# One written list of 1117 steps in place of a list of 547 steps and a scheduled rest

## The chip, the cores and the metric

The kernel runs on one core of one Trainium2 chip. The metric is device time in microseconds (us) from one run of the program. The core has five engines that work side by side, each in the order of its own instructions: TensorE (PE in the profile; its weight loads are PEld), VectorE (DVE), ScalarE (ACT), GpSimd (POOL) and SyncE (SP), which here only issues transfers (DMAs). An instruction that waits for another engine holds up what is behind it on its own engine.

## The reference, cut to what matters

A delta-rule attention over 4 batches, 8 heads, 768 tokens and 48 features feeds a feed-forward network (FFN) without a nonlinearity. The heads' outputs, side by side, are the 384 features of 3072 tokens.

```python
k_n = k / (np.linalg.norm(k, axis=-1, keepdims=True) + 1e-06)
for t in range(S):
    y[:, :, t] = q[:, :, t] @ state
    v_old = state.T @ k_n[:, :, t]
    state = state + beta[t] * outer(k_n[:, :, t], v[:, :, t] - v_old)
x = y.transpose(0, 2, 1, 3).reshape(3072, 384)
out = ((x @ w1) * (x @ w2)) @ w3 @ w_out
```

(The products over batch and head are written short here.) The weights arrive as 64-bit floats, 1024 wide in the hidden dimension; q, k, v and beta as 32-bit floats.

## The kernel before, in words

The tokens are cut into twelve chunks (m, c) of 64; two chunks make a pair (j, u). Within a chunk the recurrence is solved at once by a triangular inverse, and only a 48 x 48 state goes from chunk to chunk. The work is cut into parts, each a generator that yields after the instructions of one engine (they are collected in `parts`, L739 and following). A call of `step(name)` (L777) runs a part up to its next yield, so one step is the work of one engine. The parts, with the lines that the profile names:

- k, q, v: load the keys, queries and values of a chunk (L173); p: load keys and queries once more, with features in other partitions (L190, sixteen DMAs in two steps); beta: loads and transposes beta.
- K, Q: for chunks 0 and 1, transposes on PE (L275) with copies to KQ (L285, L287). d: for the later chunks the same on DVE (L263).
- g and N: squares of the keys on POOL and their sums on DVE (L212, L214), then the norms (fifteen small DVE instructions, L220 to L243), once a pair.
- s: the products of keys with keys and queries (L300), written out as U (DVE, L309) and PT (L327). u: stores U in 32 x 32 blocks in DRAM (Ud, L343).
- V: the inverse of a pair's blocks. POOL clears the result (L351), SP loads the blocks (Ub, L355), 31 steps of two DVE instructions follow (L369, L374), and SP stores the result (Vd, L382). For pair 0 the result lies in PSUM meanwhile, with copies on ACT.
- e: the corner. Four loads from Vd (L387), a transpose on DVE (L399), two groups of small matmuls (L408, L422) with copies on ACT (L415, L429).
- n: values times norms on POOL (L438). c: the chain of a chunk, three groups of PE products (all at L452), each followed by a DVE step: the residual R (L484), X (L494) and the next state S (L512). y: the outputs (L547), copied on ACT to xT (L568), and for odd chunks six DMAs within xT (L579).
- P: a piece of weights. SP loads it (L592), ACT works on it twice (L600, L601), DVE twice (L603, L604), POOL once (L608). P0 to P7 are w_out, P8 to P23 w3, P24 to P35 w1 and w2. t transposes w3 (L643), f folds w3 and w_out into one matrix w34 (L652).
- a: an eighth of the hidden dimension for a pair's 512 tokens (128 of each batch): product with w1 on PE (L672), copy on ACT (L681), product with w2 on PE (L672), elementwise product on DVE (L686). o: a batch's outputs, PE (L692), ACT (L698), store by SP (L701).

A part name carries its indices: a13 is pair 1, eighth 3; o02 is pair 0, batch 2; V2 is pair 2; P22 is a piece.

What sets the order: the string ORDER names 547 steps. They hold all weight pieces, transposes and folds, chunks 0 to 3, the scores and block stores of chunks 4 and 5, the inverses V0 to V2, and pair 0's a and o steps. After them `in_text_order` (L132) ties each instruction to the one before it on its engine, so these instructions keep the order of the text on each engine. The rest, chunks 4 to 11 and the FFN blocks of pairs 1 to 5, is emitted by loops with `finish`, and the tile framework's scheduler orders those instructions by its own priorities, behind the listed ones on SP's queue (`tc.issue_after(last)`). In these loops a chunk is followed by the next chunk's values and corner, after an even chunk by the whole preparation of the pair after the next and its inverse, and then by up to six FFN parts that are ready (`emit(6)`); a pair's eight a and four o parts come up once its second chunk is out. The framework adds the waits between engines from the tiles that instructions read and write, in both cases.

Buffers that tie steps together go around in fixed turns (`in_turn`): three PSUM banks for the FFN, folds and transposes (ps_f), two double banks for scores, chain and outputs (ps_w), one for the corners (ps_t), five raw buffers shared by weight pieces and the first half of a, ten slabs shared by w3, its transposes and ab, two xT.

Of the kernel before, what the change touches and what calls it, by code (L numbers as in the profile page):

```python
# [39 lines left out]
Q1 s0 Q1 g0 g0 P11 P10 t2 N0 s0 s0 s0 k2 g1 P6 s0 P6 P6 Q1 P11 P14 P14 Q1 P14 n0 t3 P6 t3  # L40
t14 P13 s0 s0 P13 P13 P14 s1 P13 s1 s1 s1 s1 s1 p2 p2 d2 P23 P23 P23 P23 d2 d2 g1 d2 P4 P4
P4 P15 u0 P4 P15 P15 P2 P2 u1 P2 t2 P7 P7 V0 V0 V0 P7 P7 t5 V0 V0 V0 P12 P12 s1 t5 p3 P12 t6
V0 V0 V0 V0 V0 V0 V0 V0 t14 V0 V0 V0 s2 t6 t15 t15 P17 g1 g1 V0 V0 V0 V0 V0 V0 V0 V0 V0 P2
f3 p3 P12 f1 f1 f1 k3 P15 t7 t7 P29 P29 P17 V0 V0 P21 V0 V0 V0 V0 s1 V0 f3 V0 f3 P16 P16 P16
s0 f7 f7 v1 f7 t4 t4 f2 f2 P21 P21 g1 P16 t8 g1 P8 V0 V0 V0 P17 P17 t9 f2 g1 P29 P29 t8 f4
P8 P8 g1 e0 e0 n0 d3 e0 P18 N1 s2 s2 s2 s2 V1 e0 e0 t9 e0 n1 n1 e1 P18 P21 t13 t13 s2 P8 t0
t0 e1 P19 P19 P20 c0 c0 e1 e1 d3 P26 P26 v3 d3 c0 c0 d3 y0 P25 y0 f4 f4 e1 P26 P26 P18 P18
c1 c1 P24 u2 P19 s3 P20 P20 t10 t10 e1 s3 s3 s3 s3 s3 f5 P19 P25 P24 P24 P20 t12 t12 P27 t11
# [2 lines left out]
P34 P28 P32 P32 P34 a03 a01 v2 V1 V1 V1 V1 V1 V1 a03 c1 a02 a01 V1 V1 g2 P32 P28 V1 P30 a03
a03 a02 a02 a02 P28 n2 V1 V1 V1 V1 V1 g2 g2 P28 P33 n3 k5 n3 a00 a01 a01 P35 p4 g2 g2 g2 a06
a00 V1 V1 V1 V1 e2 e3 n2 a06 a04 a04 a07 c1 c2 P35 P35 P33 P33 P33 a00 e2 d4 d4 P35 g2 N2 e2
e2 a04 a04 a00 e2 c2 e3 p5 d4 d4 a07 a07 a07 a06 a06 e2 s4 e3 s4 s4 s4 s4 a05 a05 a05 c2 s4
e3 e3 V2 e3 c2 c2 c2 a05 y2 y2 d5 d5 c3 p5 d5 d5 o02 c3 s5 s5 s5 o02 c3 s5 s5 u4 u5 o01 c3
# [792 lines left out]
```

## Time and profile before

| What | Value |
|---|---|
| median of 3 runs | 678.1 us (675.17 to 681.01) |
| the profiled execution's own time | 674.21 us |
| its span, first to last instruction | 672.5 us |
| mean granted clock of TensorE | 0.949 |
| busy time of PE, DVE, ACT, POOL | 597.1, 355.5, 163.2, 103.3 us |
| first FFN product (L672) starts | 142.97 us |
| last matmul ends | 668.8 us |

The trace is of one execution on the chip. A busy PE is not a PE at its peak, for matmuls overlap and their ends are modelled; what PE costs is better seen in the time from one group to the next. The granted clock is the share of full speed that the chip's throttle gave to TensorE. In a row of groups stand the line, engine, operation, output and inputs, the shape, the count, then the busy time and the mean of one in nanoseconds, then the idle time ahead of it and what ended it. The chain of waits follows the end of the program back, at each step to what released it.

### The profile page before, as it was taken

Reading aid. Unit: us, or ns where it says so; the run is one execution under the profiler, and the core shown is the slowest. Engines: PE = TensorE matmul, PEld = TensorE weight load, DVE = VectorE, ACT = ScalarE, POOL = GpSimd, SP = SyncE. Lnnn points to the kernel's source line nnn. Section 1 sums busy time; section 2 is a strip of 40 time slices with the busy share of each in tenths; the row PEclk is TensorE's granted clock in tenths of the full one; section 3 lists DMA queues with packets and bytes.
Section 4 is the critical chain, followed back from the end, with each engine's and each line's share of the span. In section 5 each row is a group of like instructions: output and inputs, shape, how many; then the busy total and the mean of one; then the engine's idle time right before and its main releaser. Section 6 shows DMA issues by size and latency. Waiting matters only on the chain.

```text
span 672.5 us, 17051 instructions
## 1 busy us (share of the span) xinstructions
PE 597.1 (89%) x7372; PEld 353.6 (53%) x7372; DVE 355.5 (53%) x764; ACT 163.2 (24%) x333; POOL 103.3 (15%) x114
## 2 busy tenths in 40 slices
PE   2627889979797999999779989999899999999997
PEld 2524467634356644556733556544656455554454
DVE  3788987789754593343497243792537822100100
ACT  2663455531312111210101220212202122201100
POOL 6374152333300102000110001100000000000000
PEclk9986977989999999899679999999899997999999
DMA  9988664786530408214551342515133020010000
GB/s 211 225 192 179 171 159 95 174 147 127 98 52 4 106 13 160 36 20 74 127 82 46 53 65 65 129 26 96 29 66 92 39 38 2 14 36 12 0 13 36
DMA packets 201835, 55.61 MB, mean 83 GB/s; under 512 B 191968, under 2 KB 195040, under 8 KB 201760
## 3 DMA queue, kind: packets, MB, share of 16 engines
q1 hardware_dynamic: 197600, 53.74, 39.1%
q10 hardware_dynamic: 4160, 0.79, 0.7%
q8 instruction: 58, 0.95, 0.6%
q14 instruction: 17, 0.14, 0.1%
HBM read 42.30 MB, written 11.01 MB: 79 GB/s over the span
## 4 chain that ended last, share of the span: by engine, by line
PE 68%; DVE 15%; DMA 6%; issue 4%; SPq 3%; ACT 2%; POOL 1%; ACTq 0%; DVEq 0%
PE ps_f L672 29%; PE ps_f L692 16%; PE ps_w L452 7%; DVE Vb L374 4%; PE ps_w L547 4%; DVE tb L369 4%; PE ps_f L652 4%; PE ps_w L300 3%; DMA ktok<-in_k_dram 2%; PE ps_t L422 2%; PE ps_t L408 2%; SPq L190 2%; DMA Ud<-U 1%; DVE w L603 1%; DVE ab L686 1%
## 5 line engine op out<-in xcount | busy, mean ns | idle before, releaser
L672 PE MATMUL ps_f<-xT,w1s 128*128 128x512 f32 x288 | 141.3, 626 | 11.5 <-DMA xT<-xT 9.6
L672 PE MATMUL ps_f<-xT,w2s 128*128 128x512 f32 x288 | 136.2, 605 | 0.2 <-DVE ab L686 0.2
L692 PE MATMUL ps_f<-w,ab 128*128 128x384 f32 x384 | 127.6, 489 | 0.0
L686 DVE TENSOR_TENSOR ab<-a,ps_f 128x512 f32<-128x512 f32 x48 | 32.7, 684 | 127.0 <-PE ps_f L672 127.0
L692 PEld LDWEIGHTS ps_f<-w,ab 128*128 128x128 f32 x384 | 72.0, 190 | 50.1 <-issue 2.9
L672 PEld LDWEIGHTS ps_f<-xT,w1s 128*128 128x128 f32 x288 | 55.1, 198 | 77.8 <-issue 64.5
L672 PEld LDWEIGHTS ps_f<-xT,w2s 128*128 128x128 f32 x288 | 54.2, 193 | 64.4 <-issue 62.5
L681 ACT COPY a<-ps_f 128x512 f32<-128x512 f32 x48 | 28.0, 586 | 185.2 <-PE ps_f L672 169.6
L369 DVE TENSOR_TENSOR tb<-Vb,Ub 128x31 f32<-128x31 f32 (+15 forms) x155 | 57.5, 371 | 15.2 <-DMA Ub<-Ud 11.0
L374 DVE TENSOR_TENSOR Vb<-Vb,tb 128x31 f32<-128x31 f32 (+15 forms) x155 | 60.6, 391 | 4.5
L438 POOL TENSOR_TENSOR vtok<-vtok,n 128x384 f32<-128x384 f32 x24 | 20.4, 868 | 196.2 <-DMA vtok<-in_v_dram 146.8
L568 ACT COPY xT<-ps_w 48x256 f32<-48x256 f32 x96 | 30.5, 366 | 74.6 <-PE ps_w L547 74.2
L652 PE MATMUL ps_f<-w2s,w3T 128*128 128x384 f32 x128 | 45.0, 503 | 2.4 <-ACT w3T L646 1.4
L698 ACT COPY osb<-ps_f 128x384 f32<-128x384 f32 x24 | 11.5, 479 | 121.2 <-PE ps_f L692 101.5
L300 PE MATMUL ps_w<-KQ 48*64 48x128 f32 x768 | 32.0, 315 | 6.0 <-ACT PT L321 4.9
L309 DVE TENSOR_TENSOR U<-ps_w,wt 128x512 f32<-128x512 f32 x24 | 16.4, 686 | 38.6 <-PE ps_w L300 38.4
L212 POOL TENSOR_TENSOR sq<-ktok 128x384 f32<-128x384 f32 x24 | 21.4, 894 | 89.5 <-DVE ss L214 33.9
L494 DVE TENSOR_TENSOR X<-ps_w,wt 128x384 f32<-128x384 f32 x24 | 12.3, 552 | 42.6 <-PE ps_w L452 42.6
L652 PEld LDWEIGHTS ps_f<-w2s,w3T 128*128 128x128 f32 x128 | 24.2, 196 | 19.1 <-ACT w3T L646 2.2
L300 PEld LDWEIGHTS ps_w<-KQ 48*64 48x64 f32 x768 | 26.8, 158 | 11.7 <-issue 5.5
L452 PEld LDWEIGHTS ps_w<-R,TT 64*64 64x64 f32 x704 | 23.7, 143 | 10.0 <-issue 3.2
L452 PE MATMUL ps_w<-R,TT 64*64 64x48 f32 x704 | 25.5, 227 | 1.1 <-DVE R L484 1.1
(83 smaller groups left out, 574.7 us busy)
## 6 DMA issues: line engine op xcount, KB each, us to landing
raw<-in_moe_w_dram SPq DMA_DIRECT2D x16, 512.0 KB, 5.0
vtok<-in_v_dram SPq DMA_DIRECT2D x24, 192.0 KB, 4.9
raw<-in_moe_w_dram SPq DMA_DIRECT2D x24, 192.0 KB, 4.3
out_dram<-osb SPq DMA_DIRECT2D x24, 192.0 KB, 2.0
ktok<-in_k_dram SPq DMA_DIRECT2D x22, 192.0 KB, 4.0
raw<-in_moe_w_out_dram SPq DMA_DIRECT2D x8, 384.0 KB, 5.7
Ud<-U SPq DMA_DIRECT2D x48, 64.0 KB, 1.9
Ub<-Ud SPq DMA_DIRECT2D x6, 512.0 KB, 3.5
```

The source lines that it names most:

```text
L212: pool.tensor_tensor(out=sq[:], in0=kt[:, r], in1=kt[:, r], op=ALU.mult)
L300: pe.matmul(ps[half(z), h % 2, 128 * (h // 2) : 128 * (h // 2) + 128], lhsT=x[:, 0, :], rhs=x.rearrange("p j t -> p (j t)"), start=True, s ...
L369: dve.tensor_tensor(out=tv, in0=V[:, 0 : s + 1, s : s + 1].to_broadcast([P, s + 1, n]), in1=U[:, s, s + 1 : BS].unsqueeze(1).to_broadcast( ...
L374: dve.tensor_tensor(out=o, in0=o, in1=tv, op=ALU.subtract)
L452: pe.matmul(out(ps, r, h, z), lhsT=lhs(r, h, z), rhs=rhs(r, h, z), start=True, stop=True,)
L547: i = pe.matmul(region(h, z, r), lhsT=lhs, rhs=rhs, start=part[n] not in part[:n], stop=part[n] not in part[n + 1 :],)
L568: act.copy(out=xT[f, p:NP:2, b : b + NR, cc, :].rearrange("p a r t -> p r a t"), in_=pyv[f, z, b : b + NR],)
L652: pe.matmul(ps[:, 0:DM], lhsT=w3Ts[jc, kc // 4][:, kc % 4 * P : kc % 4 * P + P], rhs=wo[:, kc], start=(kc == 0), stop=(kc == KF - 1),)
L672: pe.matmul(ps[:], lhsT=w[:, m, js], rhs=x[:, m].rearrange("p b c t -> p (b c t)"), start=(m == 0), stop=(m == KM - 1),)
L681: act.copy(out=a[:], in_=ps[:])
L686: dve.tensor_tensor(out=t[:], in0=a[:], in1=ps[:], op=ALU.mult)
L692: pe.matmul(ps[:, 0:DM], lhsT=abs_[u, jc][:, b * P : (b + 1) * P], rhs=w34[:, jc, :], start=(jc == 0), stop=(jc == KF - 1),)
```

## The change

The list ORDER grows from 547 to 1117 steps and now names every step of every part, all twelve chunks, all inverses and all FFN blocks of all six pairs. The loops behind it, the helpers `finish` and `emit` and the rule that put the scheduled instructions behind the listed ones on SP's queue are gone. `in_text_order` runs as before, now over the whole program. The part functions are not touched. The first steps are not the old list's first steps either: the order of weight pieces, loads, inverses and folds is another from the start, and a and o parts no longer run whole one after another: a part's two products can lie far apart, with other parts' products or a chunk's steps between them.

```diff
 ORDER = """
-V0 P22 P1 k0 g0 K0 q0 P22 P22 P22 P1 P1 P1 g0 P3 g0 K0 P3 P3 k1 P3 K0 K0 K0 P0 g0 g0 P0 P0
-P0 P5 P5 beta Q0 Q0 Q0 Q0 Q0 P5 P5 v0 K1 K1 K1 K1 K1 g0 P10 P10 beta beta P10 P11 P11 q1 Q1
...
-t11 c1 c1 P27 f5 f5 P25 P25 y1 P9 P24 P9 P9 u3 V1 P27 P31 V1 V1 V1 V1 f6 P9 V1 V1 V1 V1 P34
-V1 V1 P27 y1 P30 t1 t1 f0 P31 V1 V1 k4 g2 V1 y1 V1 f6 P31 P31 f6 P32 P30 P30 p4 f0 f0 P34
...
-o02 V2 V2 V2 V2 V2 V2 o00 c3 o01 o00 o00 V2 V2 V2 V2 V2 o01 c3
+P6 P2 P10 k0 K0 q0 P6 P6 P2 P2 g0 g0 K0 P6 P10 P10 g0 g0 K0 K0 K0 P2 k1 K1 K1 P3 P3 P3 q1 K1
+K1 K1 P4 P4 P4 beta beta beta g0 g0 P11 P11 P11 P10 g0 g0 N0 P4 P11 Q0 Q0 Q0 P3 Q0 Q0 p2 Q1
...
+c1 e1 c1 c1 P26 P29 P29 u3 V1 k4 V1 V1 P29 f0 t11 V1 V1 V1 V1 t9 t9 P24 s1 y1 c1 f0 P27 P27
+P27 v2 n2 V1 V1 V1 V1 V1 y1 f4 P30 P30 P25 f5 f5 P32 P29 P27 f4 f4 P32 y1 g2 P30 P31 V1 c1
...
+e3 v5 e3 g2 g2 P34 N2 s4 n5 s4 P34 P34 a05 a05 c2 c2 P35 a06 s4 s4 s4 p5 p5 e3 e3 c2 c2 y2
...
+g3 a04 c3 c3 a06 n4 y3 y3 o01 o01 V2 u5 V2 V2 o00 o00 V2 V2 V2 V2 V2 V2 V2 V2 y3 a11 a11 V2
+a13 a17 a17 g3 o00 k7 V2 o01 V2 V2 V2 V2 p6 g3 V2 V2 a13 V2 V2 V2 g3 g3 V2 V2 a17 a17 V2 V2
+g3 a13 a13 a16 a16 V2 V2 d6 d6 p7 V2 V2 V2 V2 V2 o02 o02 V2 e4 e5 d6 N3 o03 o03 o03 a10 e4
...
+a10 a15 a15 u6 u7 V3 V3 a12 a12 a12 a12 y5 y5 c5 y5 o02 o12 o12 o12 V3 V3 V3 V3 V3 n6 n6 V3
+o10 o10 V3 V3 V3 V3 c5 k9 V3 d8 d8 a20 a20 o13 o13 V3 V3 V3 a24 a24 k8 V3 o10 V3 V3 g4 d8 v7
+V3 V3 V3 a27 a27 o11 o11 a22 V3 V3 a23 a23 V3 V3 V3 V3 V3 V3 a22 V3 V3 V3 e6 e6 e6 e7 c6 g4
...
+v8 V4 V4 o21 V4 V4 V4 V4 V4 V4 V4 V4 V4 V4 V4 V4 o21 V4 o22 a37 o22 a37 a34 a34 V4 V4 k10 g5
+a35 V4 V4 o21 g5 g5 V4 g5 g5 o20 o20 p10 V4 V4 V4 V4 V4 p10 V4 o22 g5 a35 o23 o23 V4 V4 V4
+V4 V4 e8 e8 a36 a36 e8 c7 c8 a35 a35 e8 e8 a31 o23 n8 o20 n8 c8 e8 e9 e9 a31 a31 a31 e9 e9
...
+V5 V5 V5 o32 o32 V5 V5 V5 V5 V5 V5 o32 V5 a47 o31 a41 V5 V5 o31 o31 a44 a44 a41 a45 a45 s11
+V5 V5 o33 o33 o33 n11 n11 a42 V5 V5 V5 V5 a42 a43 V5 V5 V5 V5 V5 V5 V5 o30 V5 V5 V5 V5 o30
+a43 e10 c9 e10 e11 e11 o30 e10 a44 e10 e10 e10 c9 c10 c10 a45 a45 c10 c10 a44 e11 e11 a46
...
+o51 o51 o51 o50 o50 o50 o52 o52 o52
 """
...
-    def finish(*names):
-        for name in names:
-            if name not in running:
-                running[name] = parts[name]()
-            for _ in running[name]:
-                pass
...
     in_text_order()
-    last = [i for i in nc.cur_bb.bb.instructions if i.engine == mybir.EngineType.SP][-1]
...
-    with tc.issue_after(last):
-        finish("e4")
-        for c in range(4, NCH):
-            finish(f"n{c}", f"c{c}", f"y{c}")
-            if c + 1 < NCH:
-                finish(f"v{c + 1}", f"e{c + 1}")
...
-            emit(6)
...
-        emit(len(units))
```

More of the change, by code (lines that the diff above doesn't have):

```diff
@@ L37 @@
 ORDER = """
-V0 P22 P1 k0 g0 K0 q0 P22 P22 P22 P1 P1 P1 g0 P3 g0 K0 P3 P3 k1 P3 K0 K0 K0 P0 g0 g0 P0 P0
-P0 P5 P5 beta Q0 Q0 Q0 Q0 Q0 P5 P5 v0 K1 K1 K1 K1 K1 g0 P10 P10 beta beta P10 P11 P11 q1 Q1
[L40 to L48, printed above, removed]
-t11 c1 c1 P27 f5 f5 P25 P25 y1 P9 P24 P9 P9 u3 V1 P27 P31 V1 V1 V1 V1 f6 P9 V1 V1 V1 V1 P34
@@ L50 @@
-V1 V1 P27 y1 P30 t1 t1 f0 P31 V1 V1 k4 g2 V1 y1 V1 f6 P31 P31 f6 P32 P30 P30 p4 f0 f0 P34
[L51 to L55, printed above, removed]
@@ L56 @@
-V2 V2 V2 V2 V2 V2 V2 V2 V2 V2 V2 v4 s5 V2 y3 y3 y3 V2 V2 V2 V2 V2 V2 V2 V2 o03 o03 o03 V2 V2
-o02 V2 V2 V2 V2 V2 V2 o00 c3 o01 o00 o00 V2 V2 V2 V2 V2 o01 c3
+P6 P2 P10 k0 K0 q0 P6 P6 P2 P2 g0 g0 K0 P6 P10 P10 g0 g0 K0 K0 K0 P2 k1 K1 K1 P3 P3 P3 q1 K1
+K1 K1 P4 P4 P4 beta beta beta g0 g0 P11 P11 P11 P10 g0 g0 N0 P4 P11 Q0 Q0 Q0 P3 Q0 Q0 p2 Q1
+Q1 Q1 s0 s0 s0 s0 s0 s0 Q1 Q1 t3 P7 P7 P7 P7 s0 P12 s1 s1 s1 s1 s1 s1 s1 p2 P12 d2 d2 t2 d2
+d2 P14 P22 P15 u0 P15 P12 P12 t4 u1 V0 P22 P22 P0 P14 P14 P14 t3 P15 P0 P0 V0 V0 V0 V0 V0
@@ new lines @@
+P22 t14 V0 V0 V0 V0 t4 t2 P5 P5 P1 P1 v0 P5 t6 t6 P15 t7 V0 p3 P1 P0 P1 P13 n0 V0 V0 V0 n0
+t14 V0 V0 V0 V0 P13 P13 V0 f1 P5 f1 f1 k2 g1 g1 g1 t7 V0 V0 V0 s0 f3 f3 P13 V0 f3 V0 V0 V0
+P23 p3 P23 t5 P23 P23 t5 P21 k3 P8 P8 V0 P21 g1 f2 f2 t15 t15 P20 P20 V0 V0 V0 P9 V0 V0 V0
+V0 V0 V0 V0 P9 f7 f7 f7 s2 f2 g1 g1 g1 P20 P20 P28 P28 t12 P8 P8 t0 t12 P21 v1 g1 P21 t13
+t13 d3 d3 P28 P9 V0 e0 f6 e0 t0 N1 e0 P28 e0 P18 s2 P9 P18 t1 s2 s2 s2 t1 e0 P18 e0 P16 P16
+P16 P18 f6 P16 e1 f6 P19 P19 P24 u2 c0 e1 e1 s2 t10 P24 c0 y0 c0 P19 e1 P26 e1 y0 t8 t8 P24
@@ new lines @@
+P17 t10 n1 d3 d3 P25 n1 P19 t11 s3 c0 s3 s3 s3 V1 f0 s3 s3 P17 P17 P17 c1 P26 P26 P25 f5 P25
+c1 e1 c1 c1 P26 P29 P29 u3 V1 k4 V1 V1 P29 f0 t11 V1 V1 V1 V1 t9 t9 P24 s1 y1 c1 f0 P27 P27
+P27 v2 n2 V1 V1 V1 V1 V1 y1 f4 P30 P30 P25 f5 f5 P32 P29 P27 f4 f4 P32 y1 g2 P30 P31 V1 c1
+V1 a02 P30 V1 V1 P31 P32 P32 V1 P31 a03 p4 V1 a02 V1 V1 V1 a00 a00 a01 V1 V1 P31 a03 a02 a02
+V1 V1 d4 p4 V1 k5 a00 a00 a01 P33 V1 V1 V1 V1 V1 V1 g2 g2 P33 g2 a01 a01 P35 a03 a03 v3 g2
+n3 d4 V1 e2 P33 n3 P34 a07 a07 a06 g2 d4 d4 a04 e2 e2 P35 P35 n2 c2 c2 a04 e2 s4 P33 e2 e2
@@ L58 @@
+a56 a56 a56 a57 a57 a54 a54 o40 a53 a53 a53 a53 a55 a55 a57 a57 a54 a54 a55 a55 o53 o53 o53
+o51 o51 o51 o50 o50 o50 o52 o52 o52
 """
```

24 lines of the change are left out of this document (11 added, 13 removed).

## The prediction

> **What bounds the kernel now.** I read the page's engine totals first, then the stretch view, then the chain of waits, then the queue rows of the slow places.
>
> ```profile
> span 672.5 us, 17051 instructions
> PE 597.1 (89%) x7372; PEld 353.6 (53%) x7372; DVE 355.5 (53%) x764; ACT 163.2 (24%) x333; POOL 103.3 (15%) x114
> ```
>
> TensorE (PE) is busy 89% of the span and VectorE (DVE) 53%. The stretch view shows where each of them is short of work; its columns are the stretch, its length, busy time (instructions) of PE, PEld, DVE, ACT and POOL, the granted clock, DMA share, GB/s.
>
> ```profile
> 10.00:53.70 43.70, 21.59 (x414) 18.35 (x414) 35.48 (x63) 25.91 (x49) 22.86 (x21) 0.89 0.98 215
> 53.70:79.30 25.60, 20.49 (x92) 12.54 (x92) 22.68 (x65) 9.18 (x18) 7.98 (x8) 0.85 0.82 175
> 79.30:118.70 39.40, 36.05 (x668) 27.24 (x668) 32.40 (x54) 21.08 (x41) 16.28 (x15) 0.78 0.50 125
> 118.70:143.00 24.30, 19.09 (x245) 12.70 (x245) 19.48 (x44) 12.35 (x26) 6.23 (x6) 1.00 0.83 166
> ...
> 153.50:319.00 165.50, 155.99 (x1967) 88.05 (x1965) 92.62 (x201) 31.31 (x66) 18.66 (x22) 0.99 0.38 67
> 319.00:345.00 26.00, 18.71 (x456) 14.85 (x456) 16.11 (x37) 3.53 (x11) 4.25 (x5) 0.67 0.54 123
> 345.00:474.00 129.00, 124.15 (x1514) 68.05 (x1512) 73.36 (x187) 23.56 (x49) 11.76 (x15) 1.00 0.37 66
> 474.00:485.00 11.00, 8.84 (x322) 7.71 (x322) 5.12 (x8) 4.09 (x11) 0.00 (x0) 0.84 0.20 27
> 485.00:555.00 70.00, 69.27 (x914) 39.91 (x916) 38.08 (x86) 11.47 (x24) 3.29 (x4) 1.00 0.26 59
> 555.00:575.00 20.00, 18.58 (x378) 11.31 (x367) 4.52 (x6) 4.31 (x11) 0.00 (x0) 0.83 0.01 2
> ```
>
> Two regimes. Up to 118.7 us DVE is the fuller engine where it matters: it converts the weight pieces, runs the first inverse (V0) and the chunk steps, and its gaps are 8.2 + 2.9 + 7.0 = 18.1 us. From 153.5 us PE is the limit. Its idle time in the rows from there is 9.5 + 7.3 + 4.9 + 2.2 + 0.7 + 1.4 = 26.0 us. Its clock, one minus the granted clock times the length, costs 1.7 + 8.6 + 1.8 + 3.4 = 15.5 us. Over half of that clock loss sits in one hole, 319 to 345.
>
> What the remaining PE work costs at full clock comes from undisturbed rows of the chain (start, length, group, matmuls):
>
> ```profile
> 190.80 1.03 PE ps_w L300 x32
> ...
> 374.96 1.13 PE ps_t L408 x64
> ...
> 378.01 1.13 PE ps_t L422 x64
> ...
> 412.45 1.15 PE ps_w L452 x64
> ...
> 415.08 2.00 PE ps_w L452 x64
> ...
> 418.57 0.87 PE ps_w L452 x64
> 419.44 0.93 PE ps_w L547 x62
> ...
> 420.48 1.15 PE ps_w L547 x63
> ...
> 558.37 1.33 issue
> ...
> 606.95 41.20 PE ps_f L672 x96
> 648.15 20.66 PE ps_f L692 x64
> ```
>
> The eight a parts of an FFN block hold sixteen products (96 matmuls), so one product is 41.20 / 16 = 2.575 us. An o part is 20.66 / 4 = 5.165 us. A chunk costs 2 x 1.03 for its scores (s), 2 x 1.13 for its corner (e), 1.15 + 2.00 + 0.87 = 4.02 for its chain (c) and 0.93 + 1.15 = 2.08 for its outputs (y). At 153.5 us three of 96 products are done. Left are 93 x 2.575 = 239.5, 24 x 5.165 = 124.0, ten e 22.6, ten c less one group 39.3, ten y 20.8 and eight s 16.5, together 463 us. The last matmul ends at 668.8, so 515.3 us are used and 52 us are lost: 26 idle, 15.5 clock, and about 10 at changes between small and large matmuls, which I can't attribute and leave as they are.
>
> **The change, part by part.** No instruction is added or removed, no DMA changes its size: the list holds every step of all 273 parts just as often as the parts have steps. So the work above stands, and every term is a change of order.
>
> *Start-up.* Ahead of V0's first DVE step the old list converts 15 weight pieces, the new one 12; by V0's end it is 16 in both, and ahead of chunk 3's first score step 25 in both. The first values (v0) and the third key chunk (k2) no longer stand on SP's queue ahead of V0's loads. What the parts cost DVE:
>
> ```profile
> L374 DVE TENSOR_TENSOR Vb<-Vb,tb 128x31 f32<-128x31 f32 (+15 forms) x155 | 60.6, 391 | 4.5
> L369 DVE TENSOR_TENSOR tb<-Vb,Ub 128x31 f32<-128x31 f32 (+15 forms) x155 | 57.5, 371 | 15.2 <-DMA Ub<-Ud 11.0
> L686 DVE TENSOR_TENSOR ab<-a,ps_f 128x512 f32<-128x512 f32 x48 | 32.7, 684 | 127.0 <-PE ps_f L672 127.0
> ...
> L512 DVE TENSOR_TENSOR S<-S,ps_w 48x768 f32<-48x768 f32 x20 | 19.0, 950 | 7.7 <-PE ps_w L452 7.5
> ...
> L604 DVE SCALAR_TENSOR_TENSOR w<-raw,w 128x512 uint32<-128x512 uint32 x16 | 16.4, 1023 | 0.5
> ...
> L263 DVE STREAM_TRANSPOSE KQ<-kperm 128x512 f32<-128x512 f32 x20 | 13.4, 691 | 6.7 <-DMA kperm<-in_k_dram 4.4 <-PE ps_w L547 2.1
> ...
> L214 DVE TENSOR_REDUCE ss<-sq 128x8 f32<-128x384 f32 x24 | 13.0, 541 | 3.2 <-POOL sq L212 3.2
> ...
> L603 DVE TENSOR_SCALAR w<-w 128x512 uint32<-128x512 uint32 x16 | 11.2, 703 | 15.4 <-ACT w L600 15.4
> ```
>
> A piece is 0.70 + 1.02 = 1.7 us of DVE, so three pieces put V0's start about 5 us forward; but they come back inside V0, so at its end only what was idle before can be gained. What then sets the first FFN product is the copy of the transposed activations (xT) behind chunk 1's outputs, and SP's queue:
>
> ```profile
> 120.43 2.16 SPq L343 DMA_DIRECT2D Ud<-U  x4
> 127.29 0.34 SPq L355 DMA_DIRECT2D Ub<-Ud  x1
> 127.67 6.87 SPq L592 DMA_DIRECT2D raw<-in_moe_w_dram  x12
> 135.30 1.32 SPq L173 DMA_DIRECT2D ktok<-in_k_dram  x2
> 136.79 5.90 SPq L579 DMA_DIRECT2D xT<-xT  x6
> ...
> 142.97 7.08 PE L672 MATMUL ps_f<-xT,w1s 128*128 128x512 f32 x12 [4.76 <-DMA xT<-xT]
> ```
>
> SP stood 4.7 us at the load of V1's input (Ub, 127.29), since that load waits for chunk 3's blocks, and twelve piece DMAs and k4 went ahead of xT. In the new list the same stand is there, and k4, v2 and three pieces still go between; so the queue is no shorter, and the gain is how much sooner chunk 3's scores are done. If DVE had no gap, that would be the whole 18 us less what the last pieces cost; if it keeps every gap, nothing; and if a piece waits for its raw buffer ahead of xT, a loss, which I bound by one more set of twelve piece DMAs, 6.9 us. I take **10 us**, about half of the gaps, because the moved pieces fill the gaps ahead of V0 and behind it, while the loads that feed them are not faster.
>
> *From the first FFN product on.* The old order ran out of FFN work: between 319 and 345 chunk 5's chain and outputs stand bare, since pair 1's FFN parts are used up and pair 2's need chunk 5's outputs. The new list hands FFN work out around each inverse and each chunk. I add up, for each inverse V2 to V5, what PE has to do between the last output ahead of it and the corner that needs it, against DVE's work and the transfers behind it:
>
> ```profile
> Vd<-Vb SPq DMA_DIRECT2D x6, 512.0 KB, 2.7
> TT<-Vd SPq DMA_DIRECT2D x48, 64.0 KB, 2.4
> ```
>
> An inverse is 31 x (0.391 + 0.371) = 23.6 us of DVE, and its way to the corner 2.7 + 2.4, 1.0 of issue (my estimate from these rows) and a transpose of 0.7, 6.8 us in all.
> V2: PE has o01, o00, o02, o03 and seven products, 20.7 + 18.0 = 38.7. DVE has the state 1.9, a06, a17 and a13 at 0.68 each, V2, three sums of 0.54 and two transposes of 0.69, 30.5, and 6.8 behind: 37.3. Slack 1.4 us.
> V3: four o and five products, 33.5; DVE from the same point has the state, the last twenty of V3's steps and three transposes, 19.2 + 6.8 = 26. Slack 7.5 us.
> V4: y7, one group of 0.87, four o and four products, 33.9; DVE 23.6 + 1.6 + 6.8 = 32. Slack 1.9 us.
> V5: four o, six products and a group of 0.87, 37.0; DVE 25.7 + 6.8 = 32.5. Slack 4.5 us.
> All four hold, two barely. Inside the chunk clusters I find one wait that no filler covers: chunk 2's third group needs a DVE step that stands behind the norms, about 2.5 us. Runs of over 300 small matmuls remain once or twice a pair, with the "issue" gap (1.33 above). So I put the remaining idle time at 2.5 for that cluster, 2.5 for the others, 2 x 2 for the thin inverses and five pairs at 1.33, 15.7 us, against 26.0: **10 us** gained. The bounds are 6.7 (the gaps alone) and 28 (each of the four inverses late by a further 6.8 us, less its slack).
>
> *The clock.* The 8.6 us of the hole go with the hole; 5.2 us stood in 474 to 485 and 555 to 575, around runs of small matmuls that the new list keeps, and I leave 5.5: **10 us** gained. The bounds are 0 left and all 15.5 left. The Trainium skill (TensorE: Matmul & The Clock Gate, Part 1) says the clock falls only after an idle window of about 3.4 us. The rows above differ: it fell to 0.83 in a stretch with 1.4 us idle in all. By the page nothing would be left to lose, and this term would be 15.5.
>
> *The end.* The last two blocks' a and o steps run back to back in both; the final copy and store lie behind the last matmul in both (3.7 us of the span). Nothing changes.
>
> The sum: 672.5 - 10 - 10 - 10 = 642.5 us span. The profiled execution took 674.2 for a span of 672.5, and the runs' median is 678.1, 0.58% above it: (642.5 + 1.7) x 1.0058 = **648 us**.
>
> **The rivals.**
> *Only the start-up changes.* The scheduler had already hidden the inverses at 345 to 474 and later: 4.9 us idle in 129. If the fixed order loses as much there in new places as it saves in the hole, 10 us remain: 662.5 span, 668 us. For it: the thin slacks. Against it: no stretch of the list lacks FFN work as 319 to 345 did.
> *Nothing measurable.* Start-up is held by the loads (0.98 of the DMA engines in 10 to 53.7) and the rest as before: 671 to 685.
> *Slower: SP's queue holds the inverses up.* V2's store (Vd) and the corner's loads stand behind sixteen loads for chunks 6 and 7 (p6.1, p7.0), V4's behind p10 and an output. Such loads wait for DVE to free their tile:
>
> ```profile
> SPq L190 <- DVE KQ L263: 37.8, 5, 19.1
> ```
>
> That is 37.8 us in five waits, the longest 19.1. In the new order PE can't go on to what stands behind the corner. It decides once a store leaves over 1.4 us (V2) or 1.9 us (V4) after its inverse. If the longest wait fell on each of these two, less slack, 35 us would be lost, and one such wait at the first FFN load besides would make 54: against the 30 gained, 672.5 + 24 = 696.5 span, about 702 us; at half the strength the two cancel. Against it: d6.0 and d6.1, which free p7.0's tile, stand five steps ahead of V2's end.
> *Deeper.* Only the "issue" gaps stay (idle 6.7, gain 19.3), no clock is lost after 153.5 (15.5), start-up gains 12: 47 us, 625.5 span, 631 us. For it: in 485 to 555 the old kernel already ran so. The clock rule of that page would be part of it.
>
> **How the numbers follow.** Forecast 648, its own range 634 to 659: 0.50. Only the start-up, 659 to 671: 0.16. Deeper, under 634: 0.13. Nothing, 671 to 685: 0.09. Slower: 0.12. A measurement of this kernel can tell about 1%, 6.8 us, so faster is 0.50 + 0.16 + 0.13 = 0.79, same 0.09, slower 0.12. The range for 8 in 10 runs from 622, somewhat below the deeper case, to 676, into the case of nothing.
>
> **What would show it.** Right, if the first FFN product starts near 133 us instead of 143; if no stretch of 26 us after it has a granted clock under 0.8; if PE's idle time from there to its last matmul is near 16 us; and if PE's last matmul ends some 30 us sooner, with the same counts of instructions. The forecast is wrong if a corner group (L408) starts behind a long wait for its transpose (L399) in any pair, if SP stands at L190 ahead of L382, or if the idle time returns as short waits for DVE at L452.

## The result, and the profile after

| | before | after |
|---|---|---|
| median | 679.56 us (675.17 to 682.12, 4 runs) | 650.32 us (646.87 to 652.74, 4 runs) |
| ratio, 95% interval | | 0.957, 0.950 to 0.964 |
| profiled execution, its span | 674.21, 672.5 us | 650.07, 648.4 us |
| mean granted clock | 0.949 | 0.953 |
| first FFN product starts | 142.97 us | 134.36 us |
| last matmul ends | 668.8 us | 644.7 us |

Faster by 4.3%, 29 us on the medians and 24.1 us between the two profiled executions. What follows is told in the profiled executions, since only they can be taken apart. All lines of the code behind the list moved down by 22: L190 is now L212, L672 is L694, L686 is L708, L399 and L408 are L421 and L430. In the kernels of the experiments the lines lie elsewhere by a few; the tiles in a row tell its group.

The page of the changed kernel, its totals:

```profile
span 648.4 us, 17045 instructions
PE 586.6 (90%) x7372; PEld 346.0 (53%) x7372; DVE 360.3 (56%) x764; ACT 162.4 (25%) x333; POOL 104.4 (16%) x114
```

The counts in the second line are the same as before; only the order differs. (The first line also counts others, 17051 before.) The start, in the trace of SP (start, length, line, transfers) and then of PE (start, length, group, and in brackets the idle time ahead of it and what ended it):

```profile
110.75 2.97 SPq L365 DMA_DIRECT2D Ud<-U  x4
115.19 0.34 SPq L377 DMA_DIRECT2D Ub<-Ud  x1
115.63 1.33 SPq L195 DMA_DIRECT2D ktok<-in_k_dram  x2
117.66 2.23 SPq L614 DMA_DIRECT2D raw<-in_moe_w_dram  x4
119.93 1.32 SPq L195 DMA_DIRECT2D vtok<-in_v_dram  x2
121.35 6.74 SPq L614 DMA_DIRECT2D raw<-in_moe_w_dram  x8
128.19 3.88 SPq L601 DMA_DIRECT2D xT<-xT  x6
```
```profile
134.36 10.46 PE L694 MATMUL ps_f<-xT,w1s 128*128 128x512 f32 x24
...
147.50 9.71 PE L694 MATMUL ps_f<-xT,w2s 128*128 128x512 f32 x22 [1.82 <-POOL w2s L630]
...
162.64 8.39 PE L694 MATMUL ps_f<-xT,w1s 128*128 128x512 f32 x12 [2.86 <-DVE ab L708]
```

The blocks of chunk 3 are stored at 110.75 and not at 120.43, and V1's load, xT and the first product follow each 9 to 12 us sooner. Four products (24 matmuls) are done at 144.7, where the old kernel had three at 153.5. Then come two waits that the old kernel did not have: 1.82 us for a weight piece that POOL hands over, and 2.86 us for DVE's product ab.

From there the stretch view, cut at the places where runs of small matmuls begin and end (columns as before):

```profile
144.70:171.00 26.30, 21.62 (x45) 8.71 (x45) 22.25 (x49) 3.54 (x6) 7.59 (x8) 0.87 0.62 131
171.00:200.00 29.00, 25.16 (x807) 19.81 (x807) 16.62 (x35) 10.20 (x21) 3.35 (x3) 0.88 0.40 57
200.00:252.00 52.00, 51.33 (x362) 27.12 (x358) 38.53 (x98) 6.69 (x16) 8.20 (x11) 1.00 0.46 89
252.00:280.00 28.00, 25.10 (x755) 17.77 (x754) 11.80 (x17) 8.36 (x18) 1.49 (x2) 0.94 0.32 52
280.00:337.00 57.00, 55.81 (x422) 30.04 (x418) 34.18 (x82) 7.38 (x17) 3.05 (x5) 1.00 0.44 85
337.00:363.00 26.00, 23.00 (x724) 16.99 (x723) 12.46 (x29) 8.27 (x18) 3.17 (x5) 0.94 0.39 66
363.00:425.00 62.00, 61.37 (x460) 32.49 (x456) 36.20 (x82) 8.36 (x19) 6.93 (x8) 0.97 0.36 73
425.00:461.00 36.00, 34.08 (x858) 22.12 (x862) 16.64 (x36) 7.87 (x18) 0.00 (x0) 0.95 0.22 32
461.00:525.00 64.00, 64.00 (x305) 32.58 (x296) 35.03 (x83) 9.04 (x20) 4.28 (x6) 1.00 0.27 60
525.00:562.00 37.00, 35.65 (x934) 23.18 (x936) 11.87 (x17) 8.74 (x19) 0.00 (x0) 1.00 0.03 8
562.00:644.70 82.70, 82.70 (x245) 42.61 (x234) 5.41 (x8) 10.56 (x23) 0.00 (x0) 1.00 0.06 20
```

No stretch is like the old 319 to 345 (clock 0.67) any more. The length less PE's busy time, added over the rows, is 20.2 us idle (before 26.0). One minus the clock, times the length, is 13.8 us (before 15.5). Long stretches of large products (200 to 252, 461 to 525, 562 on) lose nearly nothing; apart from V1's stretch, what is lost lies mostly in those with over 700 matmuls, nearly all small, but not in all of them (525 to 562 has 1.00). One of those that lose, in the trace of PE:

```profile
350.05 2.84 PE L694 MATMUL ps_f<-xT,w2s 128*128 128x512 f32 x6
352.82 0.94 PE L474 MATMUL ps_w<-X,ktok 64*48 64x48 f32 x64
353.69 1.20 PE L430 MATMUL ps_t<-T,U 32*32 32x32 f32 x64
354.82 0.67 PE L569 MATMUL ps_w<-KQ,S 48*48 48x64 f32 x32
355.30 0.67 PE L569 MATMUL ps_w<-PT,X 64*48 64x64 f32 x32
356.93 0.66 PE L569 MATMUL ps_w<-KQ,S 48*48 48x64 f32 x31 [0.96 <-issue]
357.37 0.22 PE L569 MATMUL ps_w<-PT,X 64*48 64x64 f32 x1
357.38 0.22 PE L569 MATMUL ps_w<-KQ,S 48*48 48x64 f32 x1
357.42 0.66 PE L569 MATMUL ps_w<-PT,X 64*48 64x64 f32 x31
358.01 1.20 PE L444 MATMUL ps_t<-TT,T 32*32 32x32 f32 x64
361.06 1.96 PE L474 MATMUL ps_w<-S,KQ 48*64 48x48 f32 x64 [1.85 <-issue]
362.95 4.65 PE L694 MATMUL ps_f<-xT,w2s 128*128 128x512 f32 x6
```

After a large product, 192 small matmuls run (64 + 64 + 32 + 32), then PE stands 0.96 us with "issue" as the reason: it waits for nothing that the profile shows. Then 128 more (31 + 1 + 1 + 31 + 64), and it stands 1.85 us. Behind that the next group takes 1.96 instead of 1.15 us and the next product 4.65 us, where one takes 2.575 at full clock. From 144.7 us on there are eleven such gaps, 0.63 to 1.98 us each, 12.6 of the 20.2 us idle. The old kernel's trace has seven, 1.09 to 1.95 us each, 10.3 of its 26.0. So the rest of the idle time, waits that mostly have a releaser, fell from 15.7 to 7.6 us, and the gaps grew by 2.3.

### The profile page after: what moved, and what is told of

Same layout as the page of the kernel before. It is cut to its first block, busy times and chain, and to the rows that moved or that the text cites. A ratio compares the mean times of both kernels' runs of the same rounds, so it can differ in the third digit from the quotient of the medians.

```text
span 648.4 us, 17045 instructions
## 1 busy us (share of the span) xinstructions
PE 586.6 (90%) x7372; PEld 346.0 (53%) x7372; DVE 360.3 (56%) x764; ACT 162.4 (25%) x333; POOL 104.4 (16%) x114
## 4 chain that ended last, share of the span: by engine, by line
PE 66%; DVE 13%; issue 7%; SPq 5%; DMA 5%; POOL 1%; ACT 1%; DVEq 0%; POOLq 0%; ACTq 0%
PE ps_f L694 35%; PE ps_f L714 16%; PE ps_w L474 6%; DVE tb L391 3%; PE ps_w L569 3%; SPq L614 3%; PE ps_w L322 2%; DVE Vb L396 2%; PE ps_t L444 2%; DMA raw<-in_moe_w_dram 2%; PE ps_t L430 2%; DVE ps_w L396 2%; SPq L212 1%; SPq L195 1%; DMA Vd<-Vb 1%
## 5 line engine op out<-in xcount | busy, mean ns | idle before, releaser
L694 PE MATMUL ps_f<-xT,w2s 128*128 128x512 f32 x288 | 136.3, 618 | 1.8 <-POOL w2s L630 1.8
L694 PE MATMUL ps_f<-xT,w1s 128*128 128x512 f32 x288 | 134.3, 613 | 2.9 <-DVE ab L708 2.9
L708 DVE TENSOR_TENSOR ab<-a,ps_f 128x512 f32<-128x512 f32 x48 | 32.7, 685 | 123.4 <-PE ps_f L694 113.7
L694 PEld LDWEIGHTS ps_f<-xT,w1s 128*128 128x128 f32 x288 | 55.6, 196 | 68.8 <-issue 60.7
L694 PEld LDWEIGHTS ps_f<-xT,w2s 128*128 128x128 f32 x288 | 54.7, 196 | 65.5 <-issue 61.0
L396 DVE TENSOR_TENSOR Vb<-Vb,tb 128x31 f32<-128x31 f32 (+15 forms) x155 | 62.1, 401 | 5.3
L674 PE MATMUL ps_f<-w2s,w3T 128*128 128x384 f32 x128 | 48.7, 536 | 4.3 <-POOL w2s L630 3.2
L674 PEld LDWEIGHTS ps_f<-w2s,w3T 128*128 128x128 f32 x128 | 25.8, 209 | 22.6 <-POOL w2s L630 5.8
L322 PE MATMUL ps_w<-KQ 48*64 48x128 f32 x768 | 30.1, 294 | 3.4 <-issue 2.0
L322 PEld LDWEIGHTS ps_w<-KQ 48*64 48x64 f32 x768 | 24.2, 145 | 13.5 <-issue 9.4
L630 POOL TENSOR_TENSOR w<-w,raw 128x512 uint32<-128x512 uint32 x16 | 21.2, 1332 | 29.8 <-ACT w3T L668 9.0
L506 DVE TENSOR_TENSOR R<-vtok,ps_w 128x768 f32<-128x768 f32 x11 | 10.5, 952 | 26.6 <-PE ps_w L474 21.0
```

The lines of the kernel that those rows point to most:

```text
L322: pe.matmul(ps[half(z), h % 2, 128 * (h // 2) : 128 * (h // 2) + 128], lhsT=x[:, 0, :], rhs=x.rearrange("p j t -> p (j t)"), start=True, s ...
L396: dve.tensor_tensor(out=o, in0=o, in1=tv, op=ALU.subtract)
L630: pool.tensor_tensor(out=du, in0=du, in1=lo, op=ALU.add)
L674: pe.matmul(ps[:, 0:DM], lhsT=w3Ts[jc, kc // 4][:, kc % 4 * P : kc % 4 * P + P], rhs=wo[:, kc], start=(kc == 0), stop=(kc == KF - 1),)
L694: pe.matmul(ps[:], lhsT=w[:, m, js], rhs=x[:, m].rearrange("p b c t -> p (b c t)"), start=(m == 0), stop=(m == KM - 1),)
L708: dve.tensor_tensor(out=t[:], in0=a[:], in1=ps[:], op=ALU.mult)
```

## The experiments

Where a run's idle and clock loss are named, they are PE's idle time, and one minus the granted clock times the length, added over windows of 1 us from its first FFN product to its last matmul. By that count the changed kernel has 20.2 and 13.7. e1, e2, e3 and e7 ran on one chip (before 673.63 us), e4, e5, e6 and e8 on another (before 677.45), e9 to e12 on a third (before 674.85); ratios are to the kernel before on the same chip.

**e1: the new start alone.** The new list's first 363 steps, up to its first FFN product; then the old list's remaining steps in their old order, and the old loops. (The lines are e1's against the changed kernel's.)

```diff
-P6 P2 P10 k0 K0 q0 ... P30 P31 V1 c1 V1 a02 P30 V1 V1 P31 P32 P32 ... o52 o52 o52
+P6 P2 P10 k0 K0 q0 ... P30 P31 V1 c1 V1 v3 P34 P31 V1 P31 P31 ... o01 c3
+    with tc.issue_after(last):
+        finish("e4")
+        for c in range(4, NCH):
...
```

> The new list is kept up to its first FFN product; from there the old list's remaining steps follow, and then the old loops with the scheduler. My theory: the gain of 29 us has two parts, about 11 us from the start-up (first product at 134 instead of 143, and the four first ones without a slow clock) and about 12 us from what comes after. So this kernel should take 679.6 less 11 = 668 us (664 to 672), its first FFN product should start at 133 to 136 us, and the hole with a granted clock under 0.75 should still be there. Rival A (all of it is start-up): 650 to 656. Rival B (all of it is the later order): 676 to 683, although the first product starts early.

Measured 668.38 us (665.31 to 671.75), ratio 0.991 (0.989 to 0.994), span 664.1. The first product came 9.35 us sooner, but its trace of PE goes on so:

```profile
133.62 7.89 PE L671 MATMUL ps_f<-xT,w1s 128*128 128x512 f32 x18
148.91 7.87 PE L671 MATMUL ps_f<-xT,w2s 128*128 128x512 f32 x12 [7.39 <-POOL w2s L607]
```

Three products run, and the fourth, the first with w2, stands 7.39 us for its converted weights. It starts at 148.91 and in the old kernel at 153.53, so 4.6 us are kept, as in the medians (5.2). The first product was the wrong mark for the start: the next late thing is the first w2 piece. Idle is 32.0 us and clock loss 15.4 in the whole. The hole around chunk 5 is still there by its idle time (7.6 us from 306 to 332), but not by its clock, which was expected under 0.75 and is 0.87. Ahead of chunk 5's three chain groups PE waits for DVE as in the old kernel (0.63, 1.07 and 0.66 us; there 0.62, 1.07 and 0.66). There the clock was at half from 324.0 on, at the second of these waits; in e1 it stayed at 1.00 through all three.

**e2 and e10: the old start with the new remainder.** The old list's first 367 steps, then all other steps in the new list's order. The old start loads v3 ahead of v2, the new remainder uses them the other way round; e10 mends that alone. (The lines are e10's against e2's.)

```diff
-... e1 d3 P26 P26 v3 d3 c0 c0 ... P28 P28 P28 c1 v2 n2 c1 ... P35 a03 a03 g2 n3
+... e1 d3 P26 P26 v2 d3 c0 c0 ... P28 P28 P28 c1 n2 c1 ... P35 a03 a03 v3 g2 n3
```

> The reverse: the old list up to its first FFN product, then every step that is left in the order of the new list. My theory: 650.3 plus 11 = 661 us (657 to 665), first FFN product at 141 to 145, no stretch of 26 us with a clock under 0.8 after it. Rival A (all start-up): 675 to 682. Rival B (all later): 648 to 653.

> The old start-up with the new rest once more, but with chunk 2's values loaded where the old start loads chunk 3's, so that the two value buffers take the turns that the new list was made for (it loads chunk 5's values ahead of chunk 4's). My theory: the old start with the new rest failed (674 us) since the load of chunk 5's values stood on SP till 205 us for chunk 3's residual and held up chunk 5's perm loads behind it, 5.6 us of PE's idle time and what follows; without that it should come to 664 to 668 us, 0.985 to 0.992 of before. Rival J (the new rest only fits the new start, everywhere): 0.997 or more.

e2: 674.1 us (671.84 to 677.47), ratio 1.001 (0.999 to 1.004), so the expectation missed. Its trace of SP and its waits of SP (total, times, longest), then the groups of PE:

```profile
182.72 1.02 SPq L407 DMA_DIRECT2D TT<-Vd  x2
205.51 1.33 SPq L193 DMA_DIRECT2D vtok<-in_v_dram  x2
206.88 4.59 SPq L210 DMA_DIRECT2D kperm<-in_k_dram  x8
```
```profile
SPq L193 <- DVE R L504: 37.4, 2, 21.7
```
```profile
218.92 2.27 PE L320 MATMUL ps_w<-KQ 48*64 48x128 f32 x29 [5.58 <-DVE KQ L283]
```

SP stands 21.7 us at one load of values whose buffer is still read by another chunk's residual. The key loads for later scores stand behind it, DVE's transposes behind them, and PE 5.58 us behind those. e10, the same kernel with the two loads in the order of their use, 664.91 us (661.38 to 666.97), ratio 0.985 (0.981 to 0.989), as expected:

```profile
188.90 1.32 SPq L193 DMA_DIRECT2D vtok<-in_v_dram  x2
```

The load starts 16.6 us sooner, and the difference of the ratios is worth 0.0162 x 675 = 11 us. So one load in the wrong turn can take back over a third of what the list brings. The new remainder by itself is worth 1.5% (idle 25.3, clock 15.3), the new start by itself 0.9%; together they are worth 4.3%. The parts do not add: some 13 us come only where start and remainder fit each other. Much of it stands in the traces at the seam: in e1 the 7.39 us above and 5.1 us of clock behind them, in e10 waits of 3.77 us for a copy on ACT and 3.14 us for ab among pair 0's products, with 1.7 us of clock behind each. What the rest is was not followed up.

**e7 and e11: how much the later steps need the list.** e7 keeps the new list's first 677 steps (into pair 2) and hands the rest to the old loops; e11 keeps all steps, but ties only the first 677 to the order of the text and lets the scheduler order the last 440. (The lines are e11's.)

```diff
-    for name in ORDER.split():
+    names = ORDER.split()
+    for name in names[:677]:
         step(name)
     in_text_order()
+    last = [i for i in nc.cur_bb.bb.instructions if i.engine == mybir.EngineType.SP][-1]
+    with tc.issue_after(last):
+        for name in names[677:]:
+            step(name)
```

> The new list up to the first FFN product of pair 2 (677 steps), then the old loops with the scheduler for what is left. My theory: the later gain is the filled hole around chunk 5, and the stretches after it were good in the old kernel too, so this kernel keeps nearly all of the gain: 650 to 657 us. Rival C (the gain is spread over all pairs, each fixed order a little better than the scheduler's): a third to a half of the later 12 us is lost, 658 to 664. Rival A and B don't differ here.

> The changed kernel's list, with fixed edges on its first 677 steps alone (up to the first product of pair 2); the other 440 steps are given to the scheduler in the list's order, behind the fixed ones on SP's queue. My theory: PE has enough work in every later stretch, so the scheduler can lose little there, and what was lost without any edges (722 us) was lost in the start-up and around V1: 650 to 660 us, 0.960 to 0.974 of before. Rival D (the scheduler undoes a good order wherever it is): 668 us or more, 0.987. Rival E (the edges cost): 0.955 or less.

e7: 657.52 us (654.02 to 658.56), ratio 0.976 (0.972 to 0.980), idle 25.5, clock 8.5; that is just above the 650 to 657 expected. e11, as expected: 653.4 us (647.86 to 654.71), ratio 0.967 (0.962 to 0.972), idle 24.6, clock 11.9. So the list up to pair 2 brings 2.4 of the 4.3%, the order of the later steps 0.9 more, and fixing them on each engine may bring the rest (the intervals of e11 and of the changed kernel overlap).

**e3: the list without its fixed order.** All 1117 steps, and no `in_text_order`.

```diff
     for name in ORDER.split():
         step(name)
-    in_text_order()
```

> The new list of 1117 steps without the edges that fix each engine's order: the scheduler sees the steps in the new order and may deviate. My theory: what counts is which step stands ready where, so the order of the text brings most of it, and the free scheduler loses some: 652 to 666 us. Rival D (the fixed edges are the point, the scheduler undoes a good order by its own priorities): 668 us or more. Rival E (the fixed edges cost, the scheduler mends thin places such as the wait for a01's product at 162.6): 640 to 649 us.

722.3 us (720.5 to 724.48), ratio 1.073 (1.069 to 1.077). The trace of PE:

```profile
199.43 2.08 PE L694 MATMUL ps_f<-xT,w2s 128*128 128x512 f32 x2 [20.07 <-ACT a L703]
```

Its first product starts at 168.79, 34 us later than in the changed kernel, and 20.07 us are lost soon after. The list is a list for engines that keep its order: the same steps, freely scheduled, are slower than the kernel before. My expectation (652 to 666 us) missed, and the rival by which the fixed order is the point came true, though e11 limits it to the steps before pair 2's products.

**e8, e4, e9: the runs of small matmuls.** e8 is the changed kernel again. e4 moves mostly single FFN products so that from pair 1 on no more than 192 small matmuls follow one another. e9 is e4 with five more moves, among them two of pair 1's steps earlier beside V2.

```diff
-... s6 s6 c4 e5 e5 c4 c4 c4 a11 a11 c4 y4 y4 c4 ... p8 s7 s7 s7 a14 a14 a14 s7 s7 s7 a15 a15
+... s6 s6 a11 c4 e5 e5 c4 c4 a14 a14 c4 a11 c4 y4 a14 y4 c4 ... p8 s7 a15 s7 s7 a14 s7 s7 s7 a15
...
-... a13 V2 V2 V2 g3 g3 V2 V2 a17 a17 V2 V2 g3 a13 a13 a16 a16
+... a13 V2 a17 a17 a13 V2 V2 g3 g3 V2 V2 a13 V2 V2 g3 a16 a16
```

(The first pair of lines is e4's against the changed kernel's, the second e9's against e4's.)

> The changed kernel itself once more, as the reference for the three kernels beside it. Every theory: 0.950 to 0.965 of the kernel before, with about 20 us idle and 14 us of clock lost after the fourth FFN product.

> Only FFN products are moved within the new list, so that no run of small matmuls between two large ones is longer than 192 from pair 1 on (it was up to 480, and 320 or more in six places). My theory: the issue gaps (12.6 us in eleven places after the first FFN products) come from long runs, since the sequencer gets its next block of instructions more slowly than small matmuls use it up, and most of the 13.9 us of lost clock follows them. Then 8 to 10 us of the gaps and 4 to 8 us of the clock go: 12 to 18 us less than the changed kernel. Rival F (the gaps depend on how many small matmuls there are, not on how they lie): within 3 us of the changed kernel, with the same sum of gaps. Rival G (a moved product makes DVE or ScalarE late): the gaps go, and as much comes back as waits for DVE.

> The spread list once more, with the four new waits mended that it showed: the elementwise product of a17 sooner on DVE within V2, the scores of chunk 7 one product later, one small group between each copy of a corner (ScalarE) and the chain group that needs it, and chunk 7's state ahead of the corner of chunk 8 on DVE. My theory: the gaps it removed were real but came back as waits for DVE and ScalarE of 9 us (3.8, 1.9, 2 x 1.0 and smaller); with these gone the idle time after the first FFN product falls from 18 to about 10 us, and the time by 6 to 9 us below the changed kernel's 648.8: 0.945 to 0.950 of before. Rival I (PE was never held up by these places, DVE's inverses are, and any wait taken away shows up at the next corner): within 2 us of the changed kernel, 0.955 to 0.960.

e8: 648.78 us (647.03 to 653.17), ratio 0.958 (0.954 to 0.963), idle 20.9 with 14.7 in "issue" gaps, clock 11.9. e4: 648.17 us (644.09 to 650.02), ratio 0.956 (0.952 to 0.961), idle 17.9, clock 10.2. Its "issue" gaps are three, 2.5 us. So breaking the runs removes most of the gaps. But the time hardly moved, where 12 to 18 us less were expected; it came out as the rival had it in which as much comes back as waits for DVE. In e4's trace of PE:

```profile
237.80 13.50 PE L712 MATMUL ps_f<-w,ab 128*128 128x384 f32 x32 [3.80 <-DVE ab L706]
...
282.32 2.48 PE L320 MATMUL ps_w<-KQ 48*64 48x128 f32 x32 [1.91 <-DVE KQ L283]
```

The products that now break up the runs were the cover of DVE's steps elsewhere. At and behind these two waits the clock was at half again, and 6.8 of e4's 10.2 us of clock loss lie there: waits cost clock as the gaps do. e9: 644.32 us (641.03 to 647.01), ratio 0.955 (0.951 to 0.959), span 641.0, idle 20.4 and clock 3.4. The stretch view of e9 at the old trouble spots, and its longest wait:

```profile
335.00:362.00 27.00, 25.75 (x625) 16.28 (x625) 16.50 (x35) 7.10 (x16) 5.09 (x7) 1.00 0.47 79
...
421.00:460.00 39.00, 38.22 (x911) 24.32 (x911) 17.83 (x38) 10.92 (x26) 0.00 (x0) 1.00 0.29 47
```
```profile
252.74 1.92 PE L428 MATMUL ps_t<-T,U 32*32 32x32 f32 x64 [7.54 <-DVE T L419]
```

Where the changed kernel had a clock of 0.94 and 0.95, e9 has 1.00, with 625 and 911 matmuls in the stretch. In the changed kernel the losses of these two stretches stand behind the gaps of 0.96 and 1.85 us and behind a wait of 0.76 us for DVE at 425.23; in e9 the gaps are gone and that wait is 0.53. So the clock loss there went with these stands of PE, in one trace (the mean clocks of e9's six runs are 0.952 to 0.968, this trace's is 0.965, e8's six are 0.953 to 0.960). In its place the corner of chunk 4 stands 7.54 us for V2's result: PE is there at 245.2 instead of 252.1, and the thin slack of 1.4 us that the prediction worked out for V2 is used up. e9 has the lowest median, but its ratio missed the 0.945 to 0.950 expected and its interval overlaps e8's, so it is not shown to be faster.

**e5 and e6: the waits beside V1.** e5 exchanges the weight pieces P29 and P31, so that w2's piece is ready sooner, and puts two ab products earlier on DVE (the lines show the first of these moves, against the changed kernel); e6 is e4 and e5 together. In both, a piece of w2 overwrites part of w_out in their shared memory before the last folds read it, so they fold other weights; the work is the same in kind and count.

```diff
-... c1 P26 P29 P29 u3 V1 k4 V1 V1 P29 f0 t11 ... g2 P30 P31 V1 c1 ... V1 V1 P31 P32 P32 V1 P31 a03
+... c1 P26 P31 P31 u3 V1 k4 V1 V1 P31 f0 t11 ... g2 P30 P29 V1 c1 ... V1 V1 P29 P32 P32 V1 P29 a03
```

> Two waits around V1 are taken away within the new list: the weight pieces P29 and P31 change places, so that the piece that the first w2 products need is converted sooner, and two elementwise products of pair 0 go ahead of the last steps of V1 on DVE. My theory: 1.8 + 2.9 us of PE idle go and about 1.7 us of the clock lost behind them: 4 to 7 us less than the changed kernel. Rival H (V1's end is what pair 1 waits for, and the waits come back at the corner of chunk 2): within 2 us of it.

> The moves of both kernels above together. My theory: they are at different places and add up: 16 to 24 us less than the changed kernel. If the products spread in the second stretch depend on V1's end, less: 10 to 15 us.

e5: 651.18 us (646.92 to 654.84), ratio 0.961 (0.957 to 0.966). The wait of 1.82 us for the piece is gone, and in place of the 2.86 us for ab stand two of 0.32 and 0.93. But this came a little later:

```profile
171.08 1.79 PE L428 MATMUL ps_t<-T,U 32*32 32x32 f32 x64 [3.03 <-DVE T L419]
```

PE reaches chunk 2's corner sooner, at 168.0 instead of 170.9, and stands there for V1 instead, as the rival had it. (In this trace the first product itself came 3.4 us later than in the changed kernel, at 137.78; in e6's it came at 135.02, and the wait at the corner is 3.02.) e6: 649.17 us (645.22 to 654.65), ratio 0.959 (0.954 to 0.964), idle 18.4, clock 10.2: a miss against its expectation (10 to 24 us less), and no gain over e4. So the waits around V1 moved and did not go; that DVE's total sets the pace there is my reading of it.

**e12: the hole put back.** Seven of pair 1's products are moved ahead of chunk 5's chain, so that its scores, chain and outputs stand bare.

```diff
-y4 y4 c4 c5 c5 e5 e5 p7 v6 d7 d7 p8 a14 d7 V3 d7 p8 s7 s7 s7 a14 a14 a14 s7 s7 s7 a15 a15 c5 ...
+y4 y4 c4 a14 a14 a14 a14 a15 a15 a10 a10 a15 a15 a12 a12 a12 a12 c5 c5 e5 e5 p7 v6 d7 d7 p8 d7 V3 ...
```

> The changed kernel's list with the hole put back: the seven products of pair 1 that lie between the groups of chunk 5 go ahead of them, so that chunk 5's corner, scores, chain and outputs stand bare as in the kernel before. My theory: waits for DVE between the bare groups and a slow clock, 8 to 10 us as in the old hole less its wait for xT, and V3 starts later by up to 18 us with 7.5 us of slack, 5 to 8 us more: 13 to 18 us above the changed kernel, 0.977 to 0.985 of before. Rival K (the order of the FFN products doesn't matter as long as all of them come ahead of xT): within 3 us of the changed kernel.

664.81 us (663.17 to 666.53), ratio 0.984 (0.979 to 0.989), idle 28.0, clock 25.6, as expected. Stretch view and waits:

```profile
292.80:310.00 17.20, 17.07 (x332) 14.43 (x333) 3.98 (x7) 2.54 (x8) 1.61 (x2) 0.60 0.67 98
...
340.00:352.00 12.00, 3.95 (x136) 3.89 (x140) 3.97 (x10) 2.12 (x4) 2.16 (x3) 0.67 0.53 105
```
```profile
292.73 4.18 PE L320 MATMUL ps_w<-KQ 48*64 48x128 f32 x64 [1.90 <-DVE KQ L283]
...
348.05 1.92 PE L428 MATMUL ps_t<-T,U 32*32 32x32 f32 x64 [8.20 <-DVE T L419]
```

A wait of 1.90 us for a transpose, then 17 us at a clock of 0.60 with PE all but always busy (0.40 x 17.2 = 6.9 us lost), then V3 late by 8.20 us with the clock low once more. The ratio is 2.7% above the changed kernel's, some 18 us: keeping chunk 5 covered is worth over half of the whole change, if V3's lateness, which the moved products bring about, is counted in. By the traces 7.8 us of it are idle time and 11.9 us clock.

## Why the prediction was right or wrong

**The time.** Forecast 648, measured 650.3, and 0.957 is well inside "faster". Two errors cancelled on the way. The span came down by 24.1 us, not 30. And the factor 1.0058 from the profiled execution to the median added 3.7 us that did not come: after, the two are 650.07 and 650.32. The profiled executions by themselves make a ratio of 650.07 / 674.21 = 0.964, the upper end of the interval, so 24 us is at the low side of what was gained. That 648 lies within 3 us of 650.3 is luck in part.

**Start-up: right, for more reasons than one.** The first product came 8.6 us sooner (134.4; predicted 133), and four products were done at 144.7 where three were done at 153.5: 8.8 + 2.6 = 11.4 us, against 10. The queue held as described: Ub, a key chunk, pieces and values, then xT; SP's stand ahead of Ub is there too, at 1.5 us instead of 4.7. DVE's gaps, of which the step took about half, are 6.6 + 2.1 + 1.5 = 10.2 us from 10 to 108 us, where they were 18.1 up to 118.7. What the step left out is what comes next; e1 shows it: the same early first product gives back half if the first w2 piece isn't ready.

**Idle time: somewhat over half of the gain.** 15.7 predicted, 20.2 measured, so 6 us gained and not 10. The four slacks held but for V4's, put at 1.9 us: from V2 on, the longest wait of a corner for its inverse is 0.76 us, at chunk 8; e9 and e12 show what a late one costs (7.54 and 8.20 us). The idle time outside the gaps fell by 8.1 us. But the step priced five "issue" gaps at 1.33 us, one in each pair, 6.7 us. That was already below the old kernel's seven and 10.3 us, which I had not added up; there are now eleven, 12.6 us, since a long run gives one gap after some 160 to 220 small matmuls and one more with every further 128. The waits were put at 9.0 us and came to 7.6, but in other places. The two beside V1, 4.7 us, had no term: the slacks were worked out for V2 to V5 only. At chunk 2's third group, put at 2.5 us, PE waits 0.19 us for DVE.

**The clock: this step failed.** It said that the 8.6 us of the hole go with the hole and that some more goes, 10 in all; 1.7 us went (3.6 by e8's trace of the same kernel). The hole did go, and putting it back costs 11.9 us of clock (e12). But its 8.6 us were no fixed price of that order: in e1 the hole lost 3.4. And the clock also falls at stands of 0.8 to 2.9 us, and the new order has such stands in nearly every pair. In windows of 1 us the changed kernel's loss lies in five places, each with the clock at 0.50: from 162 on at the wait of 2.86 us beside V1 (3.4 us lost), from 189 on at the gap of 1.98 (3.4), from 274 on behind the gap of 1.18 (1.7), from 360 on at the gaps of 0.96 and 1.85 (3.4), and from 428 on, 3 us behind the wait of 0.76 at 425.23 (1.7). Not every gap costs: behind 1.08 us at 303.16, 1.13 at 459.12 and 1.25 at 561.13 the clock stayed at 1.00. What decides between the two these traces do not show. The prediction had a sign of such losses in its own rows (0.83 in a stretch with 1.4 us idle) and used it only for two places. By the rule of the Trainium skill (TensorE: Matmul & The Clock Gate, Part 1), that it takes an idle window of about 3.4 us, nothing would have been lost; the trace disagrees, with a product of 4.65 us behind gaps of 0.96 and 1.85. The section of that page of the Trainium skill on a second HAM failure mode (psum-queue depth-cycling), which tells of frequent micro-idles between groups of bf16 matmuls, is nearer to these rows.

**The remainder.** The old kernel lost some 10 us at changes between small and large matmuls that I could not attribute and left as they were. After, 500.0 us for 460.4 us of work (463 less one product) leave 39.6, less 20.2 and 13.8, that is 5.6 us: about 5 us gained that no step named. The sum is then 11.4 + 5.8 + 1.7 + 5.2 = 24.1 us. The clock's two digits alone make the last two terms uncertain by 2 us or so.

**The rivals.** "Only the start-up" and "deeper" did not happen. The slower one, SP's queue, did not happen in the changed kernel, though the wait is there:

```profile
SPq L212 <- DVE KQ L285: 31.7, 3, 25.7
SPq L404 <- DVE Vb L396: 19.8, 3, 9.5
```

SP stands 25.7 us at once at a key load, longer than the 19.1 that the rival supposed, but no store of an inverse is late behind such a load by enough to show at a corner. The mark set for a wrong forecast, SP standing at L190 (now L212) ahead of an inverse's store, did come once: 9.0 us up to 240.08, right ahead of V2's store. The store left at 244.21, 1.5 us behind V2's last step, and chunk 4's corner did not wait. That such a stand can cost 11 us is shown by e2 and e10, at another load. Of the marks that the prediction set, the first product, the missing hole and the counts came out; the idle time and the last matmul (24 us sooner, not 30) fell short.

**Open.** Why changes of matmul size cost 5 us less than before was not tried. Nor was a version of e9 with V2 given back its slack; 7.5 us more is my estimate of the most it could save, from that one wait. What limits the supply in long runs is inferred, below, and why the same waits cost clock once and not another time is open.

## What to carry to other kernels

When a hole is filled from elsewhere, price what stands in every remaining run, not only in the hole: many gaps of 1 to 2 us, some with 3 to 7 us of half clock behind them, cost as much as one large hole (12.6 us of gaps here against the hole's 7.3 idle and 8.6 of clock). Work out the slack of each producer that the filler covers, and expect the wait to move to the thinnest one as soon as the gaps are gone (7.54 us in e9). A written order is one piece: its halves taken alone gave 0.9 and 1.5%, together 4.3, and one load out of its turn on a queue took 11 us.
